# Score matmuls of 64 rows by 64 columns split into two of 64 by 32 in a fused attention and feed-forward kernel

## The chip, the cores and the metric

The kernel runs on one core of a Trainium2 chip. The metric is the device time of one execution in microseconds. All data are 32-bit floats.

## What is computed

Eight batches of eight heads of attention with a threshold, on 576 positions of 64 features; its output, put together per position to 512 features, goes through a feed-forward layer of the form (x A) * (x B) W.

```python
batch, n_heads, seq, head_dim = (8, 8, 576, 64)
scores = scale * np.matmul(q, k.transpose(0, 1, 3, 2))
thresh = np.max(scores, axis=-1, keepdims=True) - tau
scores = np.where(scores >= thresh, scores, -1000000000.0)
scores = scores - np.max(scores, axis=-1, keepdims=True)
attn = np.exp(scores)
attn = attn / (np.sum(attn, axis=-1, keepdims=True) + 1e-09)
attn_out = np.matmul(attn, v)
x = attn_out.transpose(0, 2, 1, 3).reshape(B * S, H * D)   # 4608 x 512
out = (x @ w_a * (x @ w_b)) @ w_out                        # d_ff 1536
```

## The kernel before

**Pairs and units.** Two heads of a batch make a pair; a pair's features fill the 128 partitions, 64 for each head (`j`). There are 32 pairs. The queries of a pair are cut into units: `u` = 0 to 3 are 128 queries of both heads, `u` = 4 (`NT`) is the tail of 64 queries. That makes 160 units, 128 full ones and 32 tails, in the list `units` (L895 to L903).

**One unit.** `scores(i, u)` (L340) multiplies the queries by all 576 keys into PSUM banks `sc`, and DVE takes each row's maximum (L359) and the threshold (L360). `weigh` (L370) takes the exponential on ACT (L380) and masks and sums on DVE (L383). Then rows are normalised (L402 on ACT; the first eight units put the factor into a diagonal matrix, L410). The weights must be transposed for the product with v: the first eight units by PE (`turn_pe`, L427), all others by DVE in blocks of 32 (L446) and a trip through DRAM on SP's DMA queue (L457 out, L466 back). `product` (L475, matmuls at L483) multiplies with v, and `settle` (L487) copies the result to x (`xT`, L490 and L491).

**Feed-forward layer.** `ffn` (L681) is a generator that multiplies blocks of x by the weights (`plain`, L706, and with fewer multiplications `sevens_of`, L633), multiplies the two products on DVE, and multiplies with `w_out` (L763, in the first block L809). The main loop (L925) draws matmuls from it with `advance` (L843) between the steps of the attention, at a pace worked out from columns that are still to come. So PE's program is one fixed list, in which a unit's scores stand between matmuls of other lines. `keep_order` (L39) fixes the order of each engine as it was written.

**The array.** PE holds the stationary operand (for the scores: queries) and streams the moving one (keys). Where an operand covers 64 partitions and the output 64, a matmul takes one quarter of the array, called here a tile of 64*64, rows*columns as the profile writes it; its place follows from the partitions of operand and output. The feed-forward layer, the product with v and the scores all work with four such tiles. In the first 85 us there are two other forms: `prep_pe` (L333) transposes the first queries and keys with 96*128, and `turn_pe` (L427) uses 128*64.

**The scores' matmuls.** In a full unit there are eight: halves of the keys `c` (288 columns each), halves of the queries `t`, heads `j`. The head says which rows of the array, the half of the queries which columns. In the first 16 units (`BY_HEAD`) all of head 0 come first. A tail unit has four, on two tiles: head 0 on the upper columns, head 1 on the lower, so that both share one pair of banks. Each matmul of 32-bit floats that is written once stands in the profile as two weight loads and two matmuls.

Of the kernel before, what the change touches and what calls it, by code (L numbers as in the profile page):

```python
# [52 lines left out]
def kernel(  # L53
# [38 lines left out]
    nc = tc.nc  # L92
    B, H, S, D = q.shape
    P = 128
    Q = 32
# [3 lines left out]
    NT = 4  # L99
    MAIN = NT * P  # L100
# [5 lines left out]
    SH = S // 2  # L106
# [19 lines left out]
    def banks(n, name):  # L126

        return psum.tile([P, 2, 512], FP32, tag="banks", name=name)[:, :, 0:n]
# [152 lines left out]
    for _ in range(TW_BUFS):  # L281
        t = work.tile([P, 2 * NB, Q], FP32, tag="tw", bufs=TW_BUFS, name="rows")
# [57 lines left out]
    def scores(i, u):  # L340
        qT, kT = prepared[i]["q" if i < HP else "q1" if u > 1 else "q0"], prepared[i]["k"]
        base = HALF if i >= HP and u > 1 else 0
        n = 2 if u < NT else 1
        sc = [banks(SH, "sc") for _ in range(n)]
        each = [(c, t, j) for c in range(2) for t in range(n) for j in range(2)]
        if units.index((i, u)) < BY_HEAD:
            each.sort(key=lambda x: x[2])
        for c, t, j in each:
            r = slice(j * D, (j + 1) * D)
            o = t if u < NT else 1 - j  # L350
            q0, to = (u * P + t * D if u < NT else MAIN) - base, slice(o * D, (o + 1) * D)
            nc.tensor.matmul(sc[j if u < NT else 0][to, c], qT[r, q0:q0 + D],  # L352
                             kT[r, c * SH:(c + 1) * SH], start=True, stop=True)
        mx = small.tile([P, 2], FP32, tag="mx", name="mx")
        thr = small.tile([P, 2], FP32, tag="thr", name="thr")
        bias = small.tile([P, 2], FP32, tag="bias", name="bias")
        for j in range(n):
            c = slice(j, j + 1)
            nc.vector.tensor_reduce(mx[:, c], sc[j], axis=AX.XY, op=ALU.max)  # L359
        nc.vector.tensor_scalar(thr[:, 0:n], mx[:, 0:n], cut, None, op0=ALU.subtract)  # L360
        scored[i, u] = (sc, thr, bias, mx)
# [563 lines left out]
    for g in range(len(units) + PV_LAG):  # L925
# [4 lines left out]
        if here:  # L930
            i, u = units[g]
            scores(i, u)
# [125 lines left out]
```

## Time and profile before

| | |
|---|---|
| time, median of 2 runs | 1468.95 us (1465.74 to 1472.17) |
| the profiled execution: time | 1467.37 us |
| its span, first to last instruction | 1465.6 us |
| mean granted TensorE clock | 0.994 of full speed |
| L352, scores: busy, xinstructions | 192.0 us x2016, and 29.2 us x288 |
| L483, product with v: busy | 182.4 us x5184 |
| L763, product with w_out: busy | 222.9 us x3264 and 163.9 us x2448 |
| L359, DVE's maximum of the scores | 205.6 us x288, 131.3 us of waiting for L352 |

Engines are PE (matmul), PEld (PE's weight loads, beside its matmuls), DVE, ACT, POOL, and SP, whose queue moves most of the data. A group's line gives line, engine, operation, tiles, form and count, then the time in which any of the group was running, the mean length of one in ns, and the idle time of the engine ahead of them with what ended it. As tiles of the array run side by side, the lengths of single matmuls add up to more than the busy time, and groups that overlap are both counted. A matmul's recorded end is modelled. Answers by line give the least, median and greatest length of an instruction; answers in order of time give the start of a row, its length to the end of its last instruction, and how many there are.

### The profile page before, as it was taken

To read this page: it belongs to the slowest core of one execution; us is meant where nothing else is said; L and a number is where in the kernel's file an instruction comes from. 1 tells how busy PE (TensorE), PEld (TensorE's weight loads), DVE (VectorE), ACT (ScalarE), POOL (GpSimd) and SP (SyncE) were. 2 spreads that over 40 slices of the span, in tenths; PEclk is the share of its full clock that TensorE was granted. 3 is DMA by queue.
4 is the path that set the end of the run, shared out by engine and by line. 5 is a ranking of instruction groups with operands and counts; after the bars stand their busy time and mean duration, and the time that the engine had idled before them with its cause. 6 is when DMAs were issued, how large, how long until landed. Compare 5 with 4: busy or idle time off the path is not lost.

```text
span 1465.6 us, 76332 instructions
## 1 busy us (share of the span) xinstructions
PE 1387.9 (95%) x34208; PEld 1248.2 (85%) x34208; DVE 1014.9 (69%) x2245; ACT 682.9 (47%) x1243; POOL 479.5 (33%) x668
## 2 busy tenths in 40 slices
PE   5788999999999999999999899999999999999998
PEld 4677687987989889899998788998898979989997
DVE  6898688787767787586757677767767776755223
ACT  5787455545545554454444445444545455431110
POOL 2774713423060606033334224150606060605000
PEclk9999999999999999999999999999999999999999
DMA  9976677668756775577555766477656776450000
GB/s 217 227 207 181 155 183 190 167 169 189 195 135 160 165 203 145 137 174 180 142 135 138 163 165 169 121 177 167 173 147 144 179 188 165 122 148 30 4 17 17
DMA packets 325080, 223.21 MB, mean 152 GB/s; under 512 B 169616, under 2 KB 308880, under 8 KB 324752
## 3 DMA queue, kind: packets, MB, share of 16 engines
q1 hardware_dynamic: 322384, 217.73, 60.7%
q8 instruction: 269, 4.41, 1.3%
q10 hardware_dynamic: 2368, 0.59, 0.2%
q14 instruction: 59, 0.48, 0.1%
HBM read 128.58 MB, written 89.65 MB: 149 GB/s over the span
## 4 chain that ended last, share of the span: by engine, by line
PE 78%; DVE 7%; DMA 5%; SPq 5%; issue 3%; ACT 1%; POOL 1%; ACTq 0%; DVEq 0%; POOLq 0%
PE pab L633 24%; PE pab L706 18%; PE po L763 17%; PE pv L483 9%; PE sc L352 9%; DMA wT<-swap 2%; SPq L457 2%; DVE mx L359 2%; SPq L147 1%; DMA qT<-in_q_dram 1%; DVE tw L446 1%; DVE tw L383 1%; PE po L809 1%; SPq L225 1%; POOL kept L732 0%
## 5 line engine op out<-in xcount | busy, mean ns | idle before, releaser
L402 ACT ACTIVATE tw<-tw,rcp 128x576 f32<-128x576 f32 x272 | 197.8, 769 | 216.9 <-DVE rcp L396 216.8
L359 DVE TENSOR_REDUCE mx<-sc 128x1 f32<-128x576 f32 x288 | 205.6, 751 | 134.6 <-PE sc L352 131.3
L380 ACT ACTIVATE tw<-sc,bias,scalars 128x576 f32<-128x576 f32 x288 | 239.3, 831 | 9.8 <-DMA vm<-in_v_dram 0.2
L599 POOL TENSOR_TENSOR h<-h,u 128x512 f32<-128x512 f32 x28 | 35.1, 1272 | 621.8 <-DVE h L676 485.8
L383 DVE SCALAR_TENSOR_TENSOR tw<-sc,thr,tw 128x576 f32<-128x576 f32 x288 | 223.0, 798 | 14.0 <-ACT tw L380 13.8
L763 PE MATMUL po<-wo_sb,h 64*64 64x256 f32 x3264 | 222.9, 377 | 0.0
L352 PE MATMUL sc<-kT,qT 64*64 64x288 f32 x2016 | 192.0, 405 | 10.5 <-ACT xt L490 4.7
L446 DVE STREAM_TRANSPOSE tw<-tw 128x576 f32<-128x576 f32 x272 | 196.0, 754 | 0.8 <-ACT tw L402 0.8
L483 PE MATMUL pv<-wT,vm 64*64 64x160 f32 (+3 forms) x5184 | 182.4, 275 | 14.3 <-DMA wT<-swap 8.0
L763 PEld LDWEIGHTS po<-wo_sb,h 64*64 64x64 f32 x3264 | 167.4, 133 | 24.9
L483 PEld LDWEIGHTS pv<-wT,vm 64*64 64x64 f32 x5184 | 166.2, 135 | 25.3 <-issue 10.4
L763 PE MATMUL po<-sums_u,h 64*64 64x256 f32 x2448 | 163.9, 376 | 1.6 <-DVE h L714 1.6
L732 POOL TENSOR_TENSOR h<-h 128x256 f32<-128x256 f32 x168 | 117.4, 728 | 114.6 <-PE po L763 100.5
L352 PEld LDWEIGHTS sc<-kT,qT 64*64 64x64 f32 x2016 | 115.1, 133 | 32.5 <-ACT xt L490 12.3
L763 PEld LDWEIGHTS po<-sums_u,h 64*64 64x64 f32 x2448 | 123.4, 133 | 20.7 <-DVE h L714 2.3
L633 PE MATMUL pab<-xU,wb_sb 64*64 64x128 f32 x4096 | 133.5, 270 | 0.2 <-issue 0.2
L379 ACT ACTIVATE bias<-mx,scalars 128x1 f32<-128x1 f32 x288 | 83.0, 288 | 100.6 <-DVE mx L359 100.5
L633 PEld LDWEIGHTS pab<-xU,wb_sb 64*64 64x64 f32 x4096 | 127.6, 133 | 2.6 <-issue 0.5
L491 DVE COPY xT<-pv 64x128 f32<-64x128 f32 (+1 forms) x136 | 38.1, 280 | 120.3 <-PE pv L483 119.1
L633 PE MATMUL pab<-xS,wa_sb 64*64 64x128 f32 x2048 | 110.8, 270 | 3.2 <-POOL xS L506 2.0
L490 ACT COPY xT<-pv 128x128 f32<-128x128 f32 (+1 forms) x68 | 17.6, 258 | 206.0 <-PE pv L483 205.9
L706 PE MATMUL pab<-xS,wb_sb 64*64 64x256 f32 (+1 forms) x1536 | 99.9, 359 | 2.9 <-issue 2.9
(137 smaller groups left out, 2429.0 us busy)
## 6 DMA issues: line engine op xcount, KB each, us to landing
swap<-tw SPq DMA_DIRECT2D x480, 144.0 KB, 2.6
wT<-swap SPq DMA_DIRECT2D x120, 576.0 KB, 4.7
vm<-in_v_dram SPq DMA_DIRECT2D x128, 72.0 KB, 3.3
swap<-tw SPq DMA_DIRECT2D x128, 72.0 KB, 2.0
kT<-in_k_dram SPq DMA_DIRECT2D x112, 72.0 KB, 4.3
wT<-swap SPq DMA_DIRECT2D x56, 144.0 KB, 2.9
out_dram<-kept SPq DMA_DIRECT2D x30, 256.0 KB, 4.0
qT<-in_q_dram SPq DMA_DIRECT2D x112, 40.0 KB, 4.5
```

The costliest lines, as they stand in the source:

```text
L352: nc.tensor.matmul(sc[j if u < NT else 0][to, c], qT[r, q0:q0 + D], kT[r, c * SH:(c + 1) * SH], start=True, stop=True)
L359: nc.vector.tensor_reduce(mx[:, c], sc[j], axis=AX.XY, op=ALU.max)
L379: nc.scalar.activation(bias[:, j:j + 1], mx[:, j:j + 1], AF.Copy, scale=e_nscale)
L380: nc.scalar.activation(wb[j], sb[j], AF.Exp, bias=bias[:, j:j + 1], scale=e_scale)
L383: nc.vector.scalar_tensor_tensor(out=wv, in0=sb[j], scalar=thr[:, j:j + 1], in1=wv, op0=ALU.is_ge, op1=ALU.mult, accum_out=sums[:, j:j + 1])
L402: nc.scalar.activation(w, w, AF.Copy, scale=rcp[:, j:j + 1])
L446: nc.vector.transpose(w, w)
L483: nc.tensor.matmul(pv[c * D:(c + 1) * D, y], vm[rows, s], wT[y](rows, s), start=(s == 0), stop=(s == NSLOT - 1))
L633: nc.tensor.matmul(out[c * D:(c + 1) * D, r, f * P:(f + 1) * P], w[g][k][rows, w0:w0 + D], moving[k][rows], start=(fresh and k == 0 and f ...
L706: nc.tensor.matmul(pab[c * D:(c + 1) * D, r], w[rows, f // n, k, fs + c * D:fs + (c + 1) * D], moving, start=(k == 0), stop=(k == H - 1))
L732: (nc.vector if state["over"] else nc.gpsimd).tensor_tensor(*a, **kw)
L763: nc.tensor.matmul(po[c * D:(c + 1) * D, r, y], ht[rows, t0:t0 + D], other[rows, f], start=(f == 0), stop=(f == NF // 2 - 1))
```

## The change

Each matmul of the scores becomes two: the first takes the first 32 of its 64 queries, the second the other 32. Both stream the same keys, and each writes 32 partitions of the output instead of 64 (`Q` is 32). Everything else stays. Lines after it move by two: the scores' matmul is L354 in the kernel after, L483 becomes L485, L633 L635, L706 L708, L763 L765.

```diff
@@ -348,9 +348,11 @@
         for c, t, j in each:
             r = slice(j * D, (j + 1) * D)
             o = t if u < NT else 1 - j
-            q0, to = (u * P + t * D if u < NT else MAIN) - base, slice(o * D, (o + 1) * D)
-            nc.tensor.matmul(sc[j if u < NT else 0][to, c], qT[r, q0:q0 + D],
-                             kT[r, c * SH:(c + 1) * SH], start=True, stop=True)
+            q0 = (u * P + t * D if u < NT else MAIN) - base
+            for y in range(2):
+                to = slice(o * D + y * Q, o * D + (y + 1) * Q)
+                nc.tensor.matmul(sc[j if u < NT else 0][to, c], qT[r, q0 + y * Q:q0 + (y + 1) * Q],
+                                 kT[r, c * SH:(c + 1) * SH], start=True, stop=True)
```

## The prediction

> **What bounds the kernel now.** I read the page first: busy shares, the 40 slices, the chain that ended last.
>
> ```profile
> span 1465.6 us, 76332 instructions
> ...
> PE 1387.9 (95%) x34208; PEld 1248.2 (85%) x34208; DVE 1014.9 (69%) x2245; ACT 682.9 (47%) x1243; POOL 479.5 (33%) x668
> ...
> PE   5788999999999999999999899999999999999998
> ...
> PE 78%; DVE 7%; DMA 5%; SPq 5%; issue 3%; ACT 1%; POOL 1%; ACTq 0%; DVEq 0%; POOLq 0%
> ```
>
> PE is busy 95% of the span and carries 78% of the chain. Busy time by stretches puts PE at 70.3 of the first 100 us and at 1317.6 of the remaining 1366, so after the start there are only 48 us in which PE stands still. What lengthens PE's work lengthens the kernel nearly one for one. The next engine, DVE, is at 69%.
>
> Second, the instructions of the line that the change touches.
>
> ```profile
> L352 PE MATMUL sc<-kT,qT x2016: 399/402/607, 177.6 to 1302.9; 64*64 64x288 f32 x184
> L352 PE MATMUL sc<-kT,first_u x288: 402/403/739, 11.2 to 172.2; 64*64 64x288 f32 x144
> ```
>
> These 2304 are two per written matmul: 128 units of four 64-by-64 tiles have 16 each, 32 tail units on two tiles have 8 each (128 x 16 + 32 x 8 = 2304).
>
> Third, PE in order of time around one unit (start, length of the row, count).
>
> ```profile
> 869.26 1.26 PE L763 MATMUL po<-wo_sb,h 64*64 64x256 f32 x20
> 870.34 1.15 PE L352 MATMUL sc<-kT,qT 64*64 64x288 f32 x16
> 871.31 0.61 PE L763 MATMUL po<-wo_sb,h 64*64 64x256 f32 x8
> ```
>
> The reader is to see that the unit's 16 matmuls take 971 ns (870.34 to 871.31), although one lasts 402. Four tiles run side by side: four rounds of 243 ns, which is the streaming of 288 columns. Neither weights nor the change of line cost anything: the next line starts on the beat, and 402 - 243 = 159 ns of each recorded duration lie beside the tile's next matmul.
>
> Fourth, places where PE passes from one form (rows*columns of a tile) to another without waiting for data. There are only some in the first 85 us.
>
> ```profile
> 79.33 0.46 PE L483 MATMUL pv<-wT,vm 64*64 64x64 f32 x18
> ...
> 79.57 0.22 PE L483 MATMUL pv<-wT,vm 64*64 64x64 f32 x1
> 79.72 0.33 PE L427 MATMUL tp<-first_u,tw 128*64 128x128 f32 x2
> ...
> 25.15 0.28 PE L427 MATMUL tp<-first_u,tw 128*64 128x128 f32 x2
> 25.36 0.30 PE L333 MATMUL tp<-more_u,sums_u 96*128 96x96 f32 x1
> ...
> 29.06 0.22 PE L483 MATMUL pv<-wT,vm 64*64 64x64 f32 x1
> 29.21 0.30 PE L333 MATMUL tp<-more_u,sums_u 96*128 96x96 f32 x1
> ...
> 63.78 0.34 PE L706 MATMUL pab<-xS,wb_sb 64*64 64x128 f32 x4
> ```
>
> Here the new form starts about 70 ns before the recorded end of the last old matmul (79.57 + 0.22 - 79.72; 25.15 + 0.28 - 25.36; 29.06 + 0.22 - 29.21), not 159 ns before it: PE runs empty first and loses 159 - 70 = 89 ns. The first new matmuls also last longer: the two at 79.72 reach 0.33 us, some 323 ns each since they start 7 ns apart, against a median of 273 for L427. These 50 ns are their weights, loaded in the open. The case at 25.15 matters most: 128*64 to 96*128 keeps one block of rows and changes the columns, and it empties the array like the rest.
>
> **The change part by part.**
>
> *Removed and added.* 2304 matmul instructions (and as many weight loads) of 64*64 become 4608 of 64*32, each with all 288 columns of keys. In the built programs the order of the work is otherwise the same on every engine, the queues of SP and POOL included; no DMA or buffer is added.
>
> *Streaming.* A full unit has 32 instructions on eight tiles of 64 by 32. If eight run side by side that is again four rounds of 243 ns, 971 ns: cost 0. The profile shows no form with more than four tiles at once, so the bounds are 0 and eight rounds, +971 ns for each of 128 full units, +124 us. I take 0: going from two tiles of 128 rows (L427) to four of 64 rows already doubles what streams, and a round of 288 still takes its 243 ns. A tail unit uses four of the eight, two streams to each half of the rows as in before: 16 instructions, four rounds, no change. The Trainium skill ("TensorE: Matmul & The Clock Gate", Measured speedup vs the span model) reports 16 tiles of 32 by 32 at 10.6 times one; no run here shows it, and by it the streaming term would be 0 too.
>
> *Issue.* 18 matmuls with their weight loads start between 79.33 and 79.57, 13 ns for each pair. The changed unit asks for 32 in 971 ns, 30 ns each. Cost 0, hidden under the streaming; if issue were the limit, 32 x 13 = 416 ns would still fit.
>
> *Two changes of form per unit.* Before and after every group of scores come 64*64 lines (L483, L633, L706, L763). In: 89 ns of emptying and the weights of a 32-column tile in the open. These are nowhere in the profile; the nearest rows are 50 ns for 64 columns (79.72) and 59 for 128 (the 305 ns at 29.21, against the 246 that L333 has as its median). Width hardly counts, so I take 46; bounds 25 and 50. Out: 89 + 50. Sum 274 ns. Bounds: 0 if no emptying is needed between 64*64 and 64*32, and 2 x (89 + 59) = 296.
>
> The Trainium skill ("TensorE: Matmul & The Clock Gate", LDWEIGHTS) makes a weight load proportional to its columns, which would be 53 ns for 64 and 107 for 128; the rows say 50 and 59, so the measurement decides against proportion, and by the page the 32 columns would be 27 instead of 46, 3 us less in the sum. The skill's "TensorEngine Tiling (Array Packing)", Key Properties, says that a change of tiling mode drains the engine, and lists 64 by 32 as a mode of its own: the rule speaks against this change. The rows show it for the forms above and no run here shows it for 64*32; with it the sum is the one below, without it nothing.
>
> *Uneven starts.* After a change of form the tiles begin one after another, 7 ns apart (four in 0.34 us at 63.78, where one takes 0.32). Eight tiles: 47 ns; four: 20. As PE now waits for the last one, both are lost in each unit: 67 ns, in a tail unit 40. Bounds 0 and 100, since tiles also drift apart between the changes (a single L352 starts ahead of the others in many units).
>
> *Sum for PE.* Units 0 to 7 wait for DVE and ACT around their scores and partly change form already: 1 us for all. The rest: 120 full units x (274 + 67) = 40.9 us; 32 tail units x (274 + 40) = 10.0 us. Together 52 us.
>
> *What takes some of it up.* PE's waits after 100 us are short and come mostly after pv or at pab: 8.0 us for DMA wT<-swap, which started earlier and gains by a slower PE. In nine units the scores stop for 0.7 to 1.2 us after the first one or two for a bank; the change of form into them lies under that wait (9 x 135 ns = 1 us). I take 3 us back; bounds 0 and 10. DVE is later by the same 0.3 us per unit and has 31% free; its 131.3 us of waiting for the scores grow.
>
> *Total.* 1467.4 (time of the profiled execution, 1.8 above its span) + 52 - 3 = 1516. That execution lies 1.6 below the median of the runs, 1468.95, so I say 1517, 3.3% over it.
>
> **The rivals.**
>
> *Not slower: 64*64 and 64*32 don't count as different forms.* Rows stay halved and every 32-column tile lies inside one former 64-column tile, so each could follow its parent alone, as the lines follow each other at 871.31. Then streaming is equal and nothing is paid: 1467 to 1469. For it: no row shows a change between halves and quarters of the columns at equal rows. Against: 25.15, a change of columns too, at its 70 ns. It decides if a pair of changes costs under 29.4 us / 152 = 193 ns.
>
> *The four streams of one half of the rows get in each other's way.* Before has at most two. At worst each full unit needs eight rounds: 1517 + 124 = 1641, and PE would show 64*32 at twice the time per unit. For it: nothing larger than four tiles was ever seen. Against: two streams show no loss at all.
>
> *The tiles don't all get their work in time.* At 251.6 us a tail unit's two tiles take 974 ns, and in that time the other two get only about three matmuls each of the next line: PE looks ahead a few instructions per tile. With 32 in a unit, the last tiles may get theirs a round late: + 243 ns x 128 = 31 us, 1548. Against: in a full unit all four tiles start within 40 ns even where the second half of the rows stands eight matmuls later in the program (units under 16).
>
> **How the numbers follow.** Forecast 0.70, its own range 1498 to 1545: switches without the 32-column weights and with little unevenness, 152 x 0.23 - 5 = +30 us, to 152 x (0.296 + 0.1) = 60 us and 17 more, if PE's 48 us of standing still after the start grow by a third: +77. No emptying 0.12; a late round 0.08; streams in each other's way 0.08; anything else 0.02. The range reaches down to the unchanged time and up past the late round: 1464 to 1560, leaving out the eight rounds and some tail. A measurement tells about 2% from no change here: under 1498 is "same". Slower 0.84 (0.68 of the forecast + 0.08 + 0.08), same 0.15 (0.12, 0.02 of the forecast, 0.01 of the rest), faster 0.01.
>
> **What would show it.** Right: a clean full unit takes about 1.0 us from first to last start plus a gap of some 0.14 us on both sides in which no weights are loaded; the new line has 4608 matmuls at a median near 402; PE's idle time by other engines stays or shrinks; the time of L633, L706, L763, L483 does not grow. Streaming wrong: durations unchanged but about 1.9 us per unit. Emptying wrong: the next line starts on the beat after the scores, 159 ns under the recorded end. The forecast is wrong as a whole if the span grows without these gaps, or if DVE or a DMA takes over as what PE waits for.

## The result and the profile after

The changed kernel takes 1518.16 us (1517.21 to 1519.12), the kernel before 1468.95 us: ratio 1.0335, 95% interval 1.0234 to 1.0436, slower. The profiled execution takes 1519.12 us, 51.75 more than that of before; the mean granted clock is 0.994 in both.

The page of the kernel after:

```profile
span 1517.2 us, 80940 instructions
...
PE 1448.0 (95%) x36512; PEld 1108.5 (73%) x36512; DVE 1015.2 (67%) x2245; ACT 685.0 (45%) x1243; POOL 480.7 (32%) x668
...
PE 83%; DVE 5%; DMA 4%; issue 3%; SPq 2%; ACT 1%; POOL 1%; ACTq 0%; DVEq 0%; POOLq 0%
```

PE is still the bound, with 60 us more of busy time; its idle time fell from 77.7 to 69.2 us (span less busy). No other engine does more work than before. The busy share doesn't show what happened: the 95% are the same, because an array that runs empty counts as busy up to the recorded ends of its last matmuls: a pause there shows only as far as it outlasts them.

The instructions of the changed line:

```profile
L354 PE MATMUL sc<-kT,qT x4032: 399/403/428, 183.5 to 1354.7; 64*32 64x288 f32 x192
L354 PE MATMUL sc<-kT,first_u x576: 399/403/687, 11.0 to 177.6; 64*32 64x288 f32 x192
```

4608 matmuls of the old length, 403 ns at the median. PE in order of time around the same unit as the one shown of before (870.34 there):

```profile
898.83 1.20 PE L354 MATMUL sc<-kT,qT 64*32 64x288 f32 x32
899.96 0.66 PE L765 MATMUL po<-wo_sb,h 64*64 64x256 f32 x8
```

32 matmuls from 898.83 to 899.96: 1.13 us, where eight rounds of 243 ns would take 1.94. The eight tiles do stream side by side. The same place closer, with the ends of one form and the starts of the next:

```profile
898.52 0.38 PE L765 MATMUL po<-wo_sb,h 64*64 64x256 f32 x1
898.83 0.45 PE L354 MATMUL sc<-kT,qT 64*32 64x288 f32 x5
...
899.61 0.42 PE L354 MATMUL sc<-kT,qT 64*32 64x288 f32 x3
899.96 0.45 PE L765 MATMUL po<-wo_sb,h 64*64 64x256 f32 x4
```

The weight loads there, and below them those around the same unit of before:

```profile
898.83 0.67 PEld L354 LDWEIGHTS sc<-kT,qT 64*32 64x32 f32 x32 [0.39 <-DVE h L716]
899.96 0.21 PEld L765 LDWEIGHTS po<-wo_sb,h 64*64 64x64 f32 x8 [0.46 <-issue]
```

```profile
869.26 0.80 PEld L763 LDWEIGHTS po<-wo_sb,h 64*64 64x64 f32 x16
870.12 0.85 PEld L352 LDWEIGHTS sc<-kT,qT 64*64 64x64 f32 x16
871.07 0.40 PEld L763 LDWEIGHTS po<-wo_sb,h 64*64 64x64 f32 x8
```

Both changes of form start 70 ns before the recorded end of the last matmul (898.52 + 0.38 - 898.83 and 899.61 + 0.42 - 899.96), where matmuls of one form start 159 before it. It is so all along: after the first 100 us there are 149 changes into 64*32 and 149 out of it, and 147 of each stand 60 to 80 ns before that end. Weight loads stand still for 0.39 and 0.46 us, while around the unit of before no pause is over 0.10 us (870.97 to 871.07). Start times of units show the price most plainly. From the second to the third unit after 870 us of before (the same work in all kernels):

| kernel | start of unit 107, 108 (us) | apart | more than before |
|---|---|---|---|
| before | 878.02, 885.90 | 7.88 | |
| after | 906.83, 915.03 | 8.20 | 0.32 |
| e1_keys (no change of form) | 892.20, 900.09 | 7.89 | 0.01 |
| e2_half (two per unit) | 895.35, 903.55 | 8.20 | 0.32 |
| e3_four (four per unit) | 944.19, 952.72 | 8.53 | 0.65 |
| e5_wide (two per unit, with 64*128) | 887.79, 896.03 | 8.24 | 0.36 |

In the kernel after, 29 stretches from one unit to the next are longer by 0.31 to 0.33 us; the others scatter around that.

### The profile page after: what moved, and what is told of

It reads as the page before. It is cut to its first block, busy times and chain, and to the rows that moved or that the text cites. A ratio compares the mean times of both kernels' runs of the same rounds, so it can differ in the third digit from the quotient of the medians.

```text
span 1517.2 us, 80940 instructions
## 1 busy us (share of the span) xinstructions
PE 1448.0 (95%) x36512; PEld 1108.5 (73%) x36512; DVE 1015.2 (67%) x2245; ACT 685.0 (45%) x1243; POOL 480.7 (32%) x668
## 4 chain that ended last, share of the span: by engine, by line
PE 83%; DVE 5%; DMA 4%; issue 3%; SPq 2%; ACT 1%; POOL 1%; ACTq 0%; DVEq 0%; POOLq 0%
PE pab L635 26%; PE po L765 19%; PE pab L708 18%; PE sc L354 11%; PE pv L485 9%; DMA wT<-swap 2%; SPq L459 1%; DVE mx L361 1%; DVE tw L385 1%; DMA qT<-in_q_dram 1%; DVE tw L448 1%; PE po L811 1%; DMA sums_u<-in_k_dram 1%; POOL kept L734 0%; PE tp L429 0%
## 5 line engine op out<-in xcount | busy, mean ns | idle before, releaser
L361 DVE TENSOR_REDUCE mx<-sc 128x1 f32<-128x576 f32 x288 | 205.7, 751 | 169.7 <-PE sc L354 167.9
L765 PE MATMUL po<-wo_sb,h 64*64 64x256 f32 x3264 | 196.7, 378 | 0.0
L354 PE MATMUL sc<-kT,qT 64*32 64x288 f32 x4032 | 177.9, 409 | 7.3 <-issue 5.2
L485 PE MATMUL pv<-wT,vm 64*64 64x160 f32 (+3 forms) x5184 | 163.4, 273 | 7.3 <-issue 3.7
L765 PEld LDWEIGHTS po<-wo_sb,h 64*64 64x64 f32 x3264 | 126.5, 133 | 59.5 <-issue 12.1
L485 PEld LDWEIGHTS pv<-wT,vm 64*64 64x64 f32 x5184 | 152.0, 134 | 20.9 <-issue 9.0
L765 PE MATMUL po<-sums_u,h 64*64 64x256 f32 x2448 | 146.2, 377 | 1.3 <-DVE h L716 1.3
L635 PEld LDWEIGHTS pab<-xU,wb_sb 64*64 64x64 f32 x4096 | 117.0, 133 | 13.3 <-issue 10.4
L635 PE MATMUL pab<-xU,wb_sb 64*64 64x128 f32 x4096 | 124.7, 270 | 1.6 <-issue 1.6
L765 PEld LDWEIGHTS po<-sums_u,h 64*64 64x64 f32 x2448 | 95.2, 133 | 42.2 <-issue 4.6
L354 PEld LDWEIGHTS sc<-kT,qT 64*32 64x32 f32 x4032 | 70.0, 106 | 76.3 <-issue 33.7
L635 PE MATMUL pab<-xS,wa_sb 64*64 64x128 f32 x2048 | 91.7, 270 | 1.1 <-POOL xS L508 0.6
L708 PE MATMUL pab<-xS,wa_sb 64*64 64x256 f32 (+1 forms) x1536 | 90.2, 363 | 0.1
```

Of the source, the lines that this page charges most:

```text
L354: nc.tensor.matmul(sc[j if u < NT else 0][to, c], qT[r, q0 + y * Q:q0 + (y + 1) * Q], kT[r, c * SH:(c + 1) * SH], start=True, stop=True)
L485: nc.tensor.matmul(pv[c * D:(c + 1) * D, y], vm[rows, s], wT[y](rows, s), start=(s == 0), stop=(s == NSLOT - 1))
L635: nc.tensor.matmul(out[c * D:(c + 1) * D, r, f * P:(f + 1) * P], w[g][k][rows, w0:w0 + D], moving[k][rows], start=(fresh and k == 0 and f ...
L708: nc.tensor.matmul(pab[c * D:(c + 1) * D, r], w[rows, f // n, k, fs + c * D:fs + (c + 1) * D], moving, start=(k == 0), stop=(k == H - 1))
L765: nc.tensor.matmul(po[c * D:(c + 1) * D, r, y], ht[rows, t0:t0 + D], other[rows, f], start=(f == 0), stop=(f == NF // 2 - 1))
```

## The experiments

The theory at this point: each change between 64*64 and another form costs some 0.16 us, and nothing else in the change costs anything. The rival: twice as many instructions, or 32-column tiles, cost in themselves. All ratios are to the kernel before, run on the same chip; the microseconds follow from them. An undisturbed unit is one without a wait that moved, as in the table.

**e1_keys: as many instructions, no change of form**

```diff
-            nc.tensor.matmul(sc[j if u < NT else 0][to, c], qT[r, q0:q0 + D],
-                             kT[r, c * SH:(c + 1) * SH], start=True, stop=True)
+            for y in range(2):
+                ks = slice(y * SH // 2, (y + 1) * SH // 2)
+                nc.tensor.matmul(sc[j if u < NT else 0][to, c, ks], qT[r, q0:q0 + D],
+                                 kT[r, c * SH + y * SH // 2:c * SH + (y + 1) * SH // 2], start=True, stop=True)
```

> As many matmuls as in the changed kernel, but no other form: each is cut into two halves of its keys (144 columns) and stays 64*64. If the price lies in the changes of form, nothing of it is left: a unit has eight rounds of 144 columns, some 122 ns each between the 109 ns for 128 columns and the 216 for 256, that is 976 ns instead of 971, and the time is 1469 to 1472. If the price lies in the 2304 additional instructions (49 us / 2304 = 21 ns each), the time is about 1518.

Measured: 1.0181 (1.0150 to 1.0211), +26 us. Neither. Undisturbed units are 0.01 us longer, 1.5 us in all, as the first theory said. The rest comes in unequal steps, some of which go back later: from unit 20 on, 14 stretches between unit starts are longer by 1 to 4 us, 24.6 us together. All 14 hold a wait, eleven of them one put down to issue (nothing that the profile shows), mostly in L635 and L708, lines that the edit does not touch. So instructions have a price as well, but not where they stand: 25 us / 4608 = 5.4 ns each.

Two things in it are not the instructions alone. The edit puts four instructions in a row on one tile, and where all of head 0 come first, most of the first 16 units take 1.5 us from first to last start instead of 0.8; unit 20 starts 4.6 us later than in before (182.25 us, 177.62), what this costs included. And each of the three steps of about 4 us is a wait of 2.0 to 3.4 us with 3.4 us at a granted clock of 0.5 at its end or just behind it. In one of them 67 matmuls take 3.53 us, for which before needs 2.08:

```profile
367.66 3.53 PE L485 MATMUL pv<-wT,vm 64*64 64x128 f32 x67 [3.36 <-DMA wT<-swap]
```

Leaving out the first 125 us and the last 5, before has two such spells, e1_keys three and the kernel after none; each costs some 1.7 us by estimate, half of its length.

**e2_half: as many changes of form, half as many instructions**

```diff
-            for y in range(2):
-                to = slice(o * D + y * Q, o * D + (y + 1) * Q)
-                nc.tensor.matmul(sc[j if u < NT else 0][to, c], qT[r, q0 + y * Q:q0 + (y + 1) * Q],
+            w = Q if c == 0 else D
+            for y in range(D // w):
+                to = slice(o * D + y * w, o * D + (y + 1) * w)
+                nc.tensor.matmul(sc[j if u < NT else 0][to, c], qT[r, q0 + y * w:q0 + (y + 1) * w],
                                 kT[r, c * SH:(c + 1) * SH], start=True, stop=True)
```

The order by heads in the first 16 units is dropped here, in e3_four, e8_halfwide, e9_turns and e11_keys32.

> The first half of the keys with 64*32, the second with 64*64, in every unit: as many changes of form as in the changed kernel (two per unit), half as many 64*32 matmuls. If the price is that of the changes, it stays whole: 1515 to 1521, ratio about 1.033. If each 64*32 matmul or each additional instruction has a price, it halves: about 1493, ratio 1.017.

Measured: 1.0274 (1.0227 to 1.0321), +40 us, between the two. Undisturbed units are 0.32 us longer, as in the changed kernel.

**e3_four: twice as many changes of form**

```diff
+        for c, z, t, j in [(c, z, t, j) for c in range(2) for z in range(2) for t in range(n) for j in range(2)]:
...
+            w = Q if z == 0 else D
+            ks = slice(z * SH // 2, (z + 1) * SH // 2)
...
```

> Quarters of the keys (144 columns) by turns with 64*32 and 64*64: four changes of form per unit, half of the columns streamed by 64*32. If a pair of changes costs 0.32 us, wherever it stands, the price doubles: 1469 + 2 x 49 + 1 = 1568, ratio 1.067. If the price is by columns streamed through 64*32, about 1493; if by additional instructions (three halves of those in the changed kernel), 1469 + 1.5 x 49 = 1543, ratio 1.05.

Measured: 1.0763 (1.0730 to 1.0796), +112 us, and +0.65 in the undisturbed units, twice the 0.32 of two changes. The price goes with the changes of form, whatever is streamed between them.

**e4_all: no change of form, all lines with 64*32**

Every matmul of L352, L483, L633, L706, L763 and L809 is cut into two of 32 columns, as here in `plain`:

```diff
-                                nc.tensor.matmul(pab[c * D:(c + 1) * D, r],
-                                                 w[rows, f // n, k, fs + c * D:fs + (c + 1) * D], moving,
-                                                 start=(k == 0), stop=(k == H - 1))
+                                for z in range(2):
+                                    c0_ = c * D + z * Q
+                                    nc.tensor.matmul(pab[c0_:c0_ + Q, r],
+                                                     w[rows, f // n, k, fs + c0_:fs + c0_ + Q], moving,
+                                                     start=(k == 0), stop=(k == H - 1))
```

> All matmuls after the start (scores, product with v, all of the feed-forward layer) with 64*32, so that no change of form is left apart from those with the transposes of the first 85 us. If the price is that of the changes and eight tiles stream as four do, the time comes back to nearly that of before although there are twice as many matmuls: 1469 to 1490, the upper end if issuing a pair each 13.6 ns for 128 columns is too fast in places. If 64*32 matmuls cost something in themselves (21 ns for each additional one), 32000 more of them give 1469 + 670 = 2140.

Measured: 1.4911 (1.4867 to 1.4956), +718 us. The page and the waits of PE:

```profile
span 2178.3 us, 144076 instructions
...
PE 1607.8 (74%) x68080; PEld 1314.3 (60%) x68080; DVE 1013.0 (47%) x2245; ACT 690.1 (32%) x1243; POOL 480.5 (22%) x668
```

```profile
PE pab L637 <- issue: 292.1, 195, 4.0
PE pv L486 <- issue: 95.3, 72, 3.3
PE pab L712 <- issue: 63.4, 57, 3.6
...
```

PE stands still for a quarter of the span, and 528.8 us of that are waits for nothing that the profile shows (issue; 17.4 in before). They recur every 4 us or so. In the trace, there are 507 places after the first 100 us where over 0.3 us pass from one start on PE (matmul or weight load) to the next; 402 of them end 1.25 to 1.65 us after the end of a packet on the instruction queue (16 KB each, 533 of them against 269). PE gets 2 x 68080 / 2178 = 62.5 instructions per us; before ran at 2 x 34208 / 1466 = 46.7 on average. The clock was lower as well: granted 0.948 on average against 0.994, by estimate at most 113 us of PE's time (0.052 x 2178.3) against 9. So the number came out as the rival said, but most of it for another reason: PE stands still, and the place of its pauses points to a PE that runs out of instructions, not to a dearer 64*32. What that means for eight tiles in the feed-forward layer can't be read from this run.

The theory became: changes of form cost 0.16 us each, instructions cost some ns each through their supply, and PE's pauses let supply and other waits catch up, so that the two don't simply add. (By the sum, e2_half would be 48 + 2304 x 0.0054 = 60 us and not 40.)

**e5_wide and e8_halfwide: changes of form with fewer instructions**

In e8_halfwide only the first half of the keys (`c` is 0) is treated so.

```diff
-        each = [(c, t, j) for c in range(2) for t in range(n) for j in range(2)]
+        each = [(c, t, j) for c in range(2) for t in range(n) for j in range(2) if t == 0 or c not in (0, 1)]
...
-            nc.tensor.matmul(sc[j if u < NT else 0][to, c], qT[r, q0:q0 + D],
+            w = D
+            if u < NT and c in (0, 1):
+                w, to = P, slice(0, P)
+            nc.tensor.matmul(sc[j if u < NT else 0][to, c], qT[r, q0:q0 + w],
                             kT[r, c * SH:(c + 1) * SH], start=True, stop=True)
```

> The other way: the two halves of the queries of a full unit go into one matmul of 64*128 (tails stay 64*64). Streaming is equal (two tiles, four rounds of 243 ns), two changes of form in each full unit, and half as many matmuls of the scores as before. Changes alone: a clean unit is again 0.32 us longer, 120 x 0.32 = 38 us, ratio 1.026. Changes and supply of instructions: the clean unit is 0.32 us longer just the same, but 2048 PE instructions fewer save some 5 ns each and PE's own waits take up part of it, as in e2_half: 38 - 18 - 10 = +10 us, ratio 1.007.

> First half of the keys with 64*128, second with 64*64: two changes of form per full unit, a quarter fewer matmuls of the scores than before. Changes alone: +38 us as in e5_wide, ratio 1.026. Changes and supply: between e5_wide and e2_half, 38 - 18 - 5 = +15 us, ratio 1.010.

Measured: e5_wide 1.0199 (1.0155 to 1.0243), +29 us; e8_halfwide 1.0234 (1.0190 to 1.0278), +34 us. Undisturbed units are 0.36 us longer in both, 120 x 0.36 = 43 us. So 14 and 9 us are given back, less than I expected; the changes of form keep most of their price with fewer instructions than before. At 5.4 ns each, the 2048 and 1024 instructions saved would be 11 and 6 us of that, so these two runs leave little for pauses that take something up. The weights in e5_wide:

```profile
L355 PE MATMUL sc<-kT,qT x1120: 402/402/507, 179.7 to 1324.6; 64*128 64x288 f32 x151, 64*64 64x288 f32 x36
```

The first matmul after a change lasts 507 instead of 402 ns: 105 ns for 128 columns in the open, against 428 - 403 = 25 for 32 columns in the kernel after.

**e6_eighths: no change of form, three times the additional instructions**

```diff
+            for y in range(4):
+                ks = slice(y * SH // 4, (y + 1) * SH // 4)
+                nc.tensor.matmul(sc[j if u < NT else 0][to, c, ks], qT[r, q0:q0 + D],
+                                 kT[r, c * SH + y * SH // 4:c * SH + (y + 1) * SH // 4], start=True, stop=True)
```

> No change of form; each matmul of the scores is cut into four quarters of its keys (72 columns, 64*64), three times as many additional instructions as in e1_keys. Changes alone: 16 rounds of some 62 ns instead of 4 of 243, +5 us in all, ratio 1.003. Supply of instructions: three times what e1_keys lost, 3 x 25 + 5 = 80 us, ratio 1.055, in stalls at many places and not in the clean units.

Measured: 1.1249 (1.1197 to 1.1302), +183 us, more than either. The edit had a fault of its own:

```profile
462.01 2.50 PE L354 MATMUL sc<-kT,qT 64*64 64x72 f32 x59
```

59 matmuls take 2.5 us, where 16 rounds of 62 ns should take 1.0: the order puts eight instructions in a row on one tile, and the time fits two tiles at work, not four. It says nothing about supply.

**e9_turns: the same with the tiles in turns**

```diff
+        for c, t, j, y in [(c, t, j, y) for c in range(2) for y in range(4) for t in range(n) for j in range(2)]:
...
```

> As e6_eighths, but the quarters of the keys take turns over the tiles (the innermost loop of e6_eighths put eight instructions in a row on one tile, and its trace shows two tiles running instead of four). No change of form, 13824 PE instructions more than before. If e6_eighths lost its time to that order, a clean unit is now only 0.03 us longer (16 rounds of 62 ns), and what is left above +5 us is the supply of instructions: three times e1_keys, +75 us, ratio 1.05. If instructions are free, ratio 1.003.

Measured: 1.0706 (1.0656 to 1.0755), +104 us. A unit of scores, and the largest waits:

```profile
933.57 1.34 PE L351 MATMUL sc<-kT,qT 64*64 64x72 f32 x63
```

```profile
PE pab L632 <- issue: 48.6, 43, 3.6
PE sc L351 <- issue: 11.1, 17, 2.1
PE pv L482 <- issue: 10.0, 7, 3.9
```

63 matmuls now take a good 1.1 us, and undisturbed units are 0.03 us longer, 5 us in all. Of the rest, 99 us, most is in stalls: waits for issue rise from 17.4 to 82.9 us. The clock takes a part too, granted 0.984 against 0.994, by estimate at most 16 us more than in before. 99 us / 13824 = 7.2 ns for each additional instruction, or 6.0 without those 16 us.

**e11_keys32: two changes of form per unit, three times the additional instructions**

```diff
+        for c, z, t, j in [(c, z, t, j) for c in range(2) for z in range(2) for t in range(n) for j in range(2)]:
...
+            ks = slice(z * SH // 2, (z + 1) * SH // 2)
...
             for y in range(2):
                 to = slice(o * D + y * Q, o * D + (y + 1) * Q)
+                nc.tensor.matmul(sc[j if u < NT else 0][to, c, ks], qT[r, q0 + y * Q:q0 + (y + 1) * Q],
+                                 kT[r, c * SH + z * SH // 2:c * SH + (z + 1) * SH // 2], start=True, stop=True)
```

> The changed kernel with each matmul cut once more into halves of its keys (144 columns, 64*32): two changes of form per unit as in the changed kernel, three times as many additional instructions. Changes alone: as the changed kernel, +50 us, ratio 1.034. Changes and supply: 50 us plus 9216 instructions at some 5 ns, +96 us, ratio 1.066.

Measured: 1.0790 (1.0749 to 1.0831), +116 us. By itself the same number of instructions cost 104 us (e9_turns), two changes per unit 48; together they cost 116, not 152. That they overlap is shown, and where: undisturbed units pay in full (0.36 us), while PE's waits for issue fall from 82.9 us in e9_turns to 64.9, its other waits from 52.5 to 42.3.

**e7_allwide: nearly everything with 64*128**

The scores as in e5_wide, and L633, L706, L763 and L809 without their loop over halves of the columns, as here in `plain`:

```diff
-                            for c in range(2):
-                                nc.tensor.matmul(pab[c * D:(c + 1) * D, r],
-                                                 w[rows, f // n, k, fs + c * D:fs + (c + 1) * D], moving,
-                                                 start=(k == 0), stop=(k == H - 1))
+                            nc.tensor.matmul(pab[:, r], w[rows, f // n, k, fs:fs + P], moving,
+                                             start=(k == 0), stop=(k == H - 1))
```

> Scores of full units and the whole feed-forward layer with 64*128, halves of columns put together; the product with v and the tails stay 64*64. Some 14000 PE matmuls fewer than before, some 220 changes of form (around the products with v and the tails). Changes alone: 220 x 0.16 = +35 us, ratio 1.024. With supply: PE's waits put down to issue (17 us in before) go as well, and what else it lost to supply: +10 or less, ratio up to 1.007. If weights of 128 columns don't hide beside 128 columns of streaming (109 ns), L633 alone adds up to 50 ns for each of its 3584 rounds, 180 us.

Measured: 1.0083 (1.0059 to 1.0108), +12 us, with 19992 matmuls for 34208. Waits for issue are 6.1 us. Its weights of 128 columns are hidden: no sign of the 180 us. The trace has 188 changes of form after the first 100 us; at the 0.36 us for two of e5_wide that is 34 us, so fewer instructions would have won some 22 us; the price of the changes was not measured apart in this kernel. It doesn't beat before.

**e10_early: only the first eight units**

```diff
+            w = Q if units.index((i, u)) < BY_PE else D
```

> Only the first eight units are split into 64*32; they stand where PE waits for other engines and partly changes form already. Price by the prediction: 1 us, ratio 1.001. If each unit cost its 0.32 us in full, 2.6 us, ratio 1.002; both are within what the runs can tell, so the trace has to say it: unit 8 starts 1 us later than before, or 2.6.

Measured: 0.9986 (0.9960 to 1.0013). The upper end is +1.9 us, so 1 us fits and 2.6 do not. The trace doesn't decide: unit 8 starts at 83.5 us in it and at 77.5 in before, but at 78.6 in the kernel after, whose first eight units are the same: the first 85 us differ by several us between executions.

## Why the prediction was right, step by step

- *Bound.* PE was the bound and stayed it; DVE only waits longer for the scores (131.3 to 167.9 us).
- *Streaming at no cost.* Right: 1.13 us per clean unit, eight tiles at once. From first to last start it is 0.80 us and not the 1.0 of the sign, which took the time of four rounds for the three between their starts (0.75 in before). The rival of streams that get in each other's way, and that of a late round, are out.
- *Emptying.* Right at both ends: 70 ns before the recorded end as predicted, some 90 ns each. The rival without emptying is out, and e3_four doubles the price by doubling the changes.
- *Weights in the open.* Mis-sized, and for a wrong reason. I took 46 ns for 32 columns because 64 and 128 columns stood at 50 and 59; it is 25. The row of L333 misled: e5_wide has 105 ns for 128 columns, so the cost goes with the columns after all (25, 51, 105). The 51 are in the kernel after too, in the first matmuls after the way out, where L635 has 320 ns as its longest against a median of 269:

```profile
L635 PE MATMUL pab<-xU,wb_sb x4096: 266/269/320, 285.1 to 1479.2; 64*64 64x128 f32 x196
```

  The Trainium skill ("TensorE: Matmul & The Clock Gate", LDWEIGHTS) had it right: its formula, columns / 1.2, gives by estimate 27, 53 and 107 ns. My sentence that the measurement decides against it was wrong: one row of another kind of matmul wasn't enough.
- *Sum of the changes.* 1.13 us less 0.971 is 0.16 us with the second emptying; with the first (0.090), the weights of the way out (0.051) and the uneven starts of four tiles (0.020) it is 0.32 us, predicted 0.34. In a tail unit the price is 0.03 us lower. 120 x 0.32 + 32 x 0.30 = 48 us, predicted 51.
- *Issue at no cost.* This step failed. I compared the rate inside one unit (13 ns per pair seen, 30 needed) and found room, but the limit works over longer stretches, in other lines. The same 4608 instructions without changes of form cost 25 us (e1_keys).
- *What the waits take up.* Also wrong: I took back 3 us. Changes and instructions together cost much less than their sum, as e2_half and e11_keys32 show. One part is visible: PE's waits for the transposed weights (DMA wT<-swap) are 8.0 us in before, 8.8 in e1_keys and 8.3 in e9_turns, but 2.6 in the kernel after and 1.7 to 4.7 in the other kernels with changes of form all along. Longer units are enough for it, without a change of form: e6_eighths has 0.6. Lines of before and of after:

```profile
PE pv L483 <- DMA wT<-swap: 8.0, 6, 2.7
PE pab L633 <- issue: 7.8, 14, 1.9
```

```profile
PE pab L635 <- issue: 14.4, 18, 2.5
PE pv L485 <- DMA wT<-swap: 2.6, 6, 0.7
```

So the total of 49 us agrees with the predicted 48 partly by luck: 48 for the changes were right, +25 for instructions was left out, and so was a give-back of about -24, but for the 3 us. The -24 is what remains of the sum and was not measured by itself. The traces show part of it. PE's waits for other engines and DMAs add up to 53.9 us in before, 46.8 in e1_keys and 31.6 in the kernel after, its waits for issue to 17.4, 23.7 and 30.9. Against e1_keys, then, 15 us went from waits for data and 5 with the three spells at half the clock, but waits for issue grew by 7: that the pauses let the supply catch up, as the theory had it, is not seen in this kernel.

What stays open: that the stalls are the fetching of PE's instructions rests on their place 1.25 to 1.65 us after packets of the instruction queue (of PE's waits for issue after the first 100 us, 13 of 21 in before, 23 of 25 in e1_keys, 23 of 34 in the kernel after, 65 of 75 in e9_turns, 368 of 393 in e4_all) and on their growth with the number of instructions; no run changed the fetching alone. Changes to 64*32 without any additional instruction were not tried.

## What to carry to other kernels

Count the changes of tile form in PE's list, not the matmuls alone: each costs about 0.16 us here (0.18 with 64*128), however little is done between two of them, and a line of finer tiles among coarser ones pays twice per visit. An instruction that hides under streaming locally still has a price when PE's list is dense over longer stretches, and a kernel that adds both pays less than the sum, so take them apart before believing an agreement in the total. A price taken from one row needs a second row of the same kind.

## What the runs showed of the hardware

- Changing between 64*64 and 64*32 or 64*128 empties the array although the rows stay halved: some 90 ns (159 less 70) from the end of streaming to the next start, each time. The rule of the Trainium skill ("TensorEngine Tiling (Array Packing)", Key Properties), that a change of mode drains and a change of tile does not, holds here too, where only the columns change.
- Eight tiles of 64*32 with 32-bit floats stream 288 columns in the time of four of 64*64; four streams read the same half of the partitions without loss.
- PE did not get above 62.5 instructions per us over a whole kernel (e4_all), and lost time well below it, with waits that stand behind instruction packets: at an average of 49 (e1_keys) and 52 (e9_turns).
- Eight instructions in a row for one tile leave other tiles without work (e6_eighths, 2.5 us against 1.1 in e9_turns for a unit).
- After the first 125 us and before the last 5, each spell of 3.4 us at a granted clock of 0.5 in before (at 598 and 837 us) and e1_keys (at 367, 545 and 924 us) stands at a wait of PE of 1.9 to 3.4 us; not every such wait has one (2.5 us at 938 us in the kernel after).
